# An attention-plus-MLP kernel: the states' readings gathered into two runs, their first layer on 512 columns, and identity transposes that nothing reads

## The chip, the cores and the metric

The kernel runs on one core of one Trainium2 chip. The metric is the device time of one execution in microseconds. The core's engines are TensorE (PE, matmuls; the profile lists its weight loads apart as PEld), VectorE (DVE), ScalarE (ACT), GpSimd (POOL, which here only builds the identity matrix) and SyncE (SP, which issues all transfers). Each works through its own queue in order and waits for the others by semaphores.

## What is computed

Eight batches of eight heads hold 512 tokens of width 64 (`x`) and 32 states of width 64 (`state`). Tokens attend to the states and states attend to the tokens; the results, 544 rows a batch of 512 columns, go through a gated MLP without a nonlinearity, (x w_a) * (x w_b) w_out, with an inner width of 1536.

```python
def _attn_ref(x, state):
    scores = scale * np.matmul(x, state.transpose(0, 1, 3, 2))
    a = softmax(scores)                      # max, exp, sum + 1e-9
    xread = np.matmul(a, state)
    scores2 = scale * np.matmul(state, x.transpose(0, 1, 3, 2))
    a2 = softmax(scores2)
    sread = np.matmul(a2, x)
    return np.concatenate([xread, sread], axis=2)

def _moe_ref(x, w_a, w_b, w_out):
    return ((x @ w_a) * (x @ w_b)) @ w_out
```

(`softmax` stands for the four lines of the original.) Everything is float32.

## The kernel before

**Precision.** Large products are made from pairs. An operand is split into a high part rounded to float32r and a low rest, and three matmuls, high by high, high by low and low by high, are added up. The weights come as 64-bit words and are put together by ACT (`pre`), DVE (`join`) and both (`run`) in `Conv`.

**The MLP of the tokens.** A batch's first layer needs no separate reading of the states: the normalised attention of the tokens (`at_h`, `at_l`) multiplies the states already projected through w_a and w_b (`p_h`, `p_l`). `VISITS` (line 32) lists which batch meets which of the six chunks of two feature tiles in which order; `SU` stands for the unit of all states, visited three times near the end. `layer1` (line 842) fills two `ab` tiles in PSUM, one for each half of the gate; ACT copies the first, DVE multiplies the second with it, and the product is split into `g_h` and `g_l`. `layer2` (line 863) follows two feature tiles later (`LAG`) and adds into `acc` tiles; the last feature tile of a visit is closed into `stg` and stored.

**The states' side.** `soft` and `moved` exponentiate a batch's scores and store them to a scratch in DRAM (`e_dram`). `reading` (line 530) fetches them in another layout (four transfers of 64 KB for each of two groups, `a2`) with the tokens (`xn`), multiplies both in 32 small float32 matmuls of 64 columns, `scaled` divides by the sums, two transposes (`turned`) turn the result and `keep` puts it into `xst`. Batch by batch, `attend` (line 916) lets a reading follow one batch behind the attention. A small float32 matmul has two records in the profile, so a reading has 64.

**The states' MLP.** `States.tokens` splits `xst` into two tiles. In `layer1` each feature tile has, for each gate half, 4 parts of depth by 3 products, 24 matmuls of 256 columns.

**The opening.** For batch 0 the scores of group 0 come from `x_raw` (PE into `ms`), those of group 1 from `stg` (PE into `ab`). ACT copies each, four identity transposes turn them, DVE and ACT make the softmax, and `at_h` and `at_l` follow. Only then can the stream of wide matmuls begin.

**The order of the work.** All calls are recorded as units and then issued in the order that the table `ORDER` (line 138) lists by number, for all engines at once:

```python
    with tc.manual_schedule():
        for i in arranged(rec.units):
            for obj, method, args, kw in rec.units[i].calls:
                getattr(obj, method)(*map(real, args), **{k: real(x) for k, x in kw.items()})
```

So each instruction has line 1078 in the profile, and groups are told apart by tiles. Tiles take their buffers from pools in that order; `ps_ab` and `ps_ms` have two banks each, `ps_acc` four.

Of the kernel before, what the change touches and what calls it, by code (L numbers as in the profile page):

```python
# [9 lines left out]
F32 = mybir.dt.float32  # L10
# [9 lines left out]
P = 128  # L20
TOK = S + NS
NG = 2
# [23 lines left out]
LATER, TWICE = 2, (3, 4)  # L46

BEHIND = 1
# [90 lines left out]
0 5 1 6 10-11 19 23 121-122 34 137 2 35 138 36 3-4 8 520-521 7 9 37 62 38 48 68 20-21 39 22 12 49 40 296 24-25 50 13  # L139
26 16 522 51 27 41 52 14 123 28 106 42 53 43 204 31 1060 17 44 63 54-56 45 57 15 46 64 58 47 70 32 65 74 59 75 525 76  # L140
66 29 77 60 523 69 107 61 67 524 18 526 71 80 108 78 206 79 124 530 109 33 125 86 110 81 30 82 205 126 83-84 1061 85
111 576 90-91 127 208 869 92-93 112 212 94 87 95 216 128 139 113 295 72 220 129 88 96 114 97 140 130 115 98 131 99 116
142 100 160 527 141 163 166 161 143 169 102 117 132 164 118 542 170 167 89 101 133 587 103 119 134 168 165 207 104 144
518 162 73 171 120 1063 135 150 528 136 200 188 145 209 590 210 529 146-147 214 1066 151 226 211 192-193 148 105 152
213 153 218 154 149 189 215 362 156 196 190 598 535 217 155 201 191 197 157 366 202 198 579 219 194 199 172 540 173
222 178 158 1062 179-180 221 232 195 370 870 223 581 174 233 175 253 235 176 582 234 177 256 184 259 159 260 181 203
236 182-183 224 237 536 257 185 227 238-239 531 240 228 532 261 241 229 254 262 225 243 230 242 255 363-364 297 231
249 378 186 368 374 244 533 258 245-246 537 534 247-248 599 263 284 250 287 264 365 288 251 265-266 836 267 367 837
187 268-269 298 271 369 384 272 300 270 578 299 281 371 290 541 291 301 285 277 286 282 372 292 588 327 373 1070
273-274 577 376 289 375 302 583 380 303 519 275 377 324 584 325 276 379 328 1079 283 390 381 278 382 304 386 391  # L150
305-306 252 393 307-308 392 309 314 318 310 279 394 311-312 385 538 313 330-331 387 332 543 315 1071 280 333 585 334
383 335 580 319 546 342 321 539 322-323 1064 544 336 395 326 591 562 329 316 354 547 388 320 346-347 358 548 348 355
349-350 563 351-352 545 560 356 337 357 338 564 339 411 552 359 340 353 341 396 549 397 343 360 412 839 398 561 344
389 399-400 568 401 317 586 345 569 402 592 414 550 361 403-404 407 1072 405 551 417 589 1073 413 789 439 406 1081 593
1080 423 408 424 565 425 594 426 596-597 427 1082 420 1068 421 418 553 415-416 595 442 409 1074 429-432 443 1083 428
1075 554 858 1084-1085 555 422 556 433 435 434 440-441 1086 436 448 419 410 449 1087 450 481 570 1065 451 557 445 452
444 475 454 476 453 446 558 472 456 455 477 437 457 1069 458-459 462-463 460-461 571 861 504 559 468 1110 572 464 1111
465-466 566 505 484-485 840 438 567 467 486 1088 600 469 293 1076 294 487 791 601 506 490 1097 603 491 602 492 825 447
830 493 604 488 478 831 479 489 482 496 473 494-495 470 474 483 497 480 828 605 471 500 498 501 606-607 502 667 790
573 507 574 611-612 668 832 575 499 613 512-513 503 608-609 826 859 610 669 614 617 621 1067 622 508 1077 827 615 1112  # L160
833 514 1090 1113 624 616 509 1078 510 618 625-626 670 633 639 619 1106 671 1089 634 511 640 635 1107 636 1091 637-638
641 620 645 642-644 1098 728 646 515 729 731 730 627 732 1099 653 672 678 673 679-680 674-676 623 1100 792 649 829 681
793 682 834 654 630 794-795 517 798 655 677 1154 628 811 629 684 657-658 809 1108 796 650 1109 651 631 683 652 647 659
632 700 685 701-702 797 703 661 688 799 706-708 704 648 800 705 662-663 810 656 814 709 664 710-712 835 660 713 1092
691 812 841 856 692 686 733 1160 1101 734 838 735 1122 736 801 737 694 842 697 847 738 845 844 698 846 843 852 699 802
725 855 739-740 803 1123 687 871 849 862 745 741 516 872 742 695 874 693 873 689 726 1125 714 743 875 744 853 696 804
722 746 761 723 854 938 813 1124 805 817 848 762 806 1093 763-764 719 1094 1155 767-769 807 1156 690 770 716 1102-1103
717 1157 765 771 766 808 939 772 718 749 941 815 724 755 1095 756 940 816 757 720 1096 851 818 750-751 850 727 1104
942 758 1227 759 1116 1162 1105 715 721 752 747 753 783 1161 748 1114 777 819 1115 778 820 784 821 779 1117 1126 892
754 773 822 1127 780-781 760 774 786 823 785 1120 824 876 1118 1163 877 1119 878 882-883 1121 1128 884 879 775 1129  # L170
857 1228 1236 1164 1130 860 863 885 1131 880-881 864 787 2160 1132 866 865 776 1146 788 1133 901 868 902 867 2171 886
888 1165 1147 887 893 1245 1134 889 2165 782 1135-1136 665 904 1148 1137 905 910 1166 906 890 907 666 999 891 1254
1149 911 1158 912-914 1159 1229-1230 915 908-909 894 916 895-897 1000 920-921 1002 1231 922 917 943 1232 898 944 1001
945 1237 903 1233 932-933 923 946 1238 899 1234 900 1239 1140 1235 947 1003 949-950 1246 1311 1247 948 951 1240 955
924 952-953 918 954 959 1241 1138 956 928 1248 1139 971 977-978 1141 1242 925 929 1151 930 1249 1243 979 1256 1150 926
934 2126 927 1142 1144 936 1143 1735 960 1255 972 2168 931 962 980-981 1257 961 935 987 973 1258 974 1250 937 919 982
975-976 1145 965 963 983 1153 968-969 1312 984 1152 970 1265 1167 1251 1004 966 1244 967 1313 1010 1263 1252 1314 1253
1315 1317 996 1005 988 1006 1264 964 1007-1008 957 1279 993-994 1266 958 995 1011-1012 1280 1013-1014 1384 1259-1260
1015 1271 1009 1272-1273 990 1261 1283 1026-1028 1016 1267 1274 989 1017 1020 985 997 1319 991 1268 1032-1034 1318
1038 1035 1169 1269 1320 1393 998 1168 1270 1287 1039 1170 1262 1282 1040 992 1281 986 1029 1288-1289 1316 1030 1290  # L180
1036 1275 1386 1321 1021-1022 1385 1031 1057 1276-1277 1387 1018 1041 1285 1037 1388 1293 1278 1048 1389-1390 1286
1049 1042 1019 1284 1043-1044 1050 1303 1187 1394 1188 1045 1304 1023 1291 1391 1322 1171 1024 1392 1172 1395
1173-1174 1396 1292 1402 1025 1175 1294 1177 1397 1178 1323 1179 1398-1399 1180 1058-1059 1400 1176 1051-1052 1401
1181-1182 1053 1183 1411 1196 1295 1305 1299 1306 1296 1197 2162 1198 1300 1054-1055 1046 1309 1056 1297 1047 1199
1298 1301 1184 1224 1403 1193 1404 1190 1302 1405 1185 1200 1310 1413 1201 1324 1202 1420 1203 1191 1326 1325 1192
1194 1421-1422 1406 1195 1436 1423 1204-1205 1424 1437 1206 2167 1307 1425-1426 1308 1207 1211 1221 1438 1222 1412
1208 2166 1209 1328 1407-1408 1414 1329-1330 1327 1409 1331 1210 1218 1212 1415 1410 1219 1186 1189 1225 1427 1468
1226 1353-1354 1416 1439 1332 1417 1430 1334 1418 1335-1336 1428 1419 1220 1347 1429 1333 1223 1431 1350-1351 1213
1441 1432 1440 1434 1433 1348-1349 1435 1442 1375 1215 1443-1444 1541 1474 1216 1445 1337 1734 1338-1340 1217 1355
1341 1381 1352 1450 2172 1214 1342 1356-1357 1469-1470 1448 1343 1480 1358 1449 1344 2163 1362 1376 1451 1543 1359  # L190
1452 1360 2373 1361 1382 1460 1368 1383 1510 1446 1378 1447 1363-1365 1453 1461 1366 1454 1463 1379 1464 1455 1380
1507 1462 1508 1481 1377 1465 1504 1483 1505 1367 1544 1345-1346 1369 1546 1458 1476 1456 1482 1372 1511 1484-1486
1491 1471 1487 1612 1488-1489 1545 1475 1490 1492-1493 1497 2382 1494-1495 1370 1542 1496 1373 1457 1374 1498 1513
1459 1501 1466 1371 1512 1499 1519 2124 1467 1506 1547 1472 1532 2125 1533 1520 1477 1673 1538-1539 1500 1509 1478
1534 1514 1473 2374 1515-1516 1535 2375 1536 1517 2376 1518 1521 1525 1522 2377 1523 1537 1613 1524 1570 1548 1526
# [144 lines left out]
def attn_moe(ctx, tc, xt, xn, sd, wl, w_out, out):  # L340
# [13 lines left out]
    proj = pool("proj", 2)  # L354
    att = pool("att", 2)
    mlp = pool("mlp", 2)
    tail = pool("tail", 8)
# [763 lines left out]
```

## Time and profile before

| | us |
|---|---|
| median of 3 runs | 669.06 |
| lowest and highest | 668.98, 669.69 |
| the profiled execution | 669.0 |
| its span, first to last instruction | 667.2 |
| PE busy | 655.5 (98%), 3760 matmul records |
| DVE busy | 425.9 (64%), 811 instructions |
| ACT busy | 377.4 (57%), 699 instructions |
| transfers | 122.71 MB in the main queue, 55.3% of 16 DMA engines' span |

Times in the profile count from the span's start. A matmul's recorded duration includes its way through the array, so neighbours overlap; what one costs in a stream is the distance of the starts. "Idle before" is the time an engine stood still ahead of an instruction, and the name behind it is what ended that.

### The profile page before, as it was taken

To read this page: it belongs to the slowest core of one execution; us is meant where nothing else is said; L and a number is where in the kernel's file an instruction comes from. 1 tells how busy PE (TensorE), PEld (TensorE's weight loads), DVE (VectorE), ACT (ScalarE), POOL (GpSimd) and SP (SyncE) were. 2 spreads that over 40 slices of the span, in tenths; PEclk is the share of its full clock that TensorE was granted. 3 is DMA by queue.
4 is the path that set the end of the run, shared out by engine and by line. 5 is a ranking of instruction groups with operands and counts; after the bars stand their busy time and mean duration, and the time that the engine had idled before them with its cause. 6 is when DMAs were issued, how large, how long until landed. Compare 5 with 4: busy or idle time off the path is not lost.

```text
span 667.2 us, 10159 instructions
## 1 busy us (share of the span) xinstructions
PE 655.5 (98%) x3760; PEld 524.8 (79%) x3760; DVE 425.9 (64%) x811; ACT 377.4 (57%) x699; POOL 0.7 (0%) x6
## 2 busy tenths in 40 slices
PE   5999999999999999999999999999999999999997
PEld 1677777778888887888787878888888888888886
DVE  5989978856743756787867876744455544564332
ACT  4886744669986777675565543533345344543321
POOL 0000000000000000000000000000000000000000
PEclk9999999999999999999999999999999999999999
DMA  9798164688789764969978733454034330341002
GB/s 314 255 303 279 61 210 142 233 261 293 263 286 335 273 189 146 305 199 294 314 260 271 241 129 128 143 190 151 7 115 155 110 111 1 120 163 49 0 1 94
DMA packets 59632, 123.34 MB, mean 185 GB/s; under 512 B 9920, under 2 KB 18112, under 8 KB 59584
## 3 DMA queue, kind: packets, MB, share of 16 engines
q1 hardware_dynamic: 59584, 122.71, 55.3%
q8 instruction: 29, 0.48, 0.3%
q14 instruction: 19, 0.16, 0.1%
HBM read 85.46 MB, written 37.22 MB: 184 GB/s over the span
## 4 chain that ended last, share of the span: by engine, by line
PE 98%; DMA 1%; SPq 0%; DVE 0%; ACT 0%; issue 0%
PE ab L1078 45%; PE acc L1078 42%; PE ms L1078 10%; DMA stg<-xt 1%; SPq L1078 0%; DVE stg L1078 0%; ACT at_h L1078 0%
## 5 line engine op out<-in xcount | busy, mean ns | idle before, releaser
L1078 PE MATMUL acc<-wo,g_h 128*128 128x512 f32 x816 | 265.1, 391 | 0.0
L1078 PEld LDWEIGHTS acc<-wo,g_h 128*128 128x128 f32 x816 | 152.1, 188 | 33.5 <-issue 2.5
L1078 PE MATMUL acc<-wo,g_l 128*128 128x512 f32 x408 | 152.4, 391 | 0.0
L1078 DVE TENSOR_TENSOR a_sb<-ab,a_sb 128x512 f32<-128x512 f32 (+1 forms) x108 | 71.0, 657 | 125.4 <-PE ab L1078 83.2
L1078 PE MATMUL ab<-at_l,p_h 128*128 128x512 f32 x384 | 148.7, 392 | 0.0
L1078 PE MATMUL ab<-at_h,p_h 128*128 128x512 f32 x384 | 147.2, 392 | 0.0
L1078 PE MATMUL ab<-at_h,p_l 128*128 128x512 f32 x384 | 147.0, 391 | 0.0
L1078 ACT COPY a_sb<-ab 128x512 f32<-128x512 f32 (+1 forms) x108 | 60.9, 564 | 113.5 <-PE ab L1078 97.9
L1078 ACT CAST g_h<-a_sb 128x512 fp32r<-128x512 f32 (+1 forms) x108 | 64.7, 599 | 64.6 <-PE acc L1078 32.6
L1078 DVE TENSOR_TENSOR g_l<-a_sb,g_h 128x512 fp32r<-128x512 f32 (+1 forms) x108 | 70.4, 654 | 37.1 <-ACT g_h L1078 25.2
L1078 PEld LDWEIGHTS acc<-wo,g_l 128*128 128x128 f32 x408 | 76.4, 188 | 15.3
L1078 PEld LDWEIGHTS ab<-at_h,p_h 128*128 128x128 f32 x384 | 72.1, 188 | 19.4 <-issue 2.1
L1078 PEld LDWEIGHTS ab<-at_h,p_l 128*128 128x128 f32 x384 | 72.1, 188 | 18.4 <-issue 3.8
L1078 PEld LDWEIGHTS ab<-at_l,p_h 128*128 128x128 f32 x384 | 72.1, 188 | 17.3 <-issue 2.5
L1078 DVE TENSOR_TENSOR p_l<-p_raw,p_h 128x512 fp32r<-128x512 f32 x72 | 47.9, 682 | 20.5 <-ACT p_h L1078 20.5
L1078 DVE SCALAR_TENSOR_TENSOR t<-t,t 128x512 int32<-128x512 int32 x60 | 41.4, 689 | 21.1 <-ACT t L1078 19.9
L1078 ACT CAST p_h<-p_raw 128x512 fp32r<-128x512 f32 x72 | 43.3, 620 | 8.3 <-PE ab L1078 4.9
L1078 ACT ACTIVATE t<-raw 128x512 f32<-128x512 f32 x42 | 28.2, 671 | 10.7 <-DMA raw<-wl 5.1
L1078 ACT COPY sw_st<-ms 128x512 f32<-128x512 f32 x40 | 22.9, 587 | 10.4 <-PE ms L1078 10.1
L1078 PE MATMUL ms<-wq,sd_h 128*128 128x512 f32 x72 | 28.1, 391 | 0.0
L1078 PE MATMUL ms<-wq,sd_l 128*128 128x512 f32 x72 | 28.0, 389 | 0.0
L1078 ACT COPY stg<-acc 128x512 f32<-128x512 f32 x34 | 19.7, 589 | 12.5 <-PE acc L1078 12.4
(121 smaller groups left out, 628.3 us busy)
## 6 DMA issues: line engine op xcount, KB each, us to landing
p_raw<-scr SPq DMA_DIRECT2D x36, 512.0 KB, 5.0
raw<-wl SPq DMA_DIRECT2D x34, 512.0 KB, 5.3
scr<-sw_st SPq DMA_DIRECT2D x40, 256.0 KB, 5.1
out<-stg SPq DMA_DIRECT2D x34, 256.0 KB, 4.8
scr<-wo SPq DMA_DIRECT2D x32, 256.0 KB, 4.4
wo<-wl SPq DMA_DIRECT2D x10, 512.0 KB, 5.9
x_raw<-xt SPq DMA_DIRECT2D x8, 576.0 KB, 5.6
raw<-w_out SPq DMA_DIRECT2D x8, 512.0 KB, 5.4
```

What stands on the lines that cost most here:

```text
L1078: getattr(obj, method)(*map(real, args), **{k: real(x) for k, x in kw.items()})
```

## The change

Four things change in the program, and the table `ORDER` is written anew for all of it.

1. `reading` takes four batches. After visit 9 (`READ`) it reads batches 0 to 3, ahead of the states' unit batches 4 to 7; the readings in `attend` go. The fetched tiles take buffers named `raw`, `sw_st`, `sd_h`, `sd_l` and `wq`. The 256 small matmul records of four batches are one unit; two batches share one bank, and their transposes come in groups of four.
2. `tokens` puts high and low part side by side, and `States.layer1` multiplies the high weights by both in one matmul of 512 columns, the low weights by the high part in one of 256. The right half of the bank holds the second product and is added to the left by an ACT copy and a DVE addition.
3. `unread` puts 13, 4, 8 and 4 transposes of the identity ahead of batch 0's two score groups and their transposes, into the bank that is overwritten next.
4. In the last visit of the states, the second row block is computed in two column halves with an `acc` tile each, closed and stored apart.

```diff
-LATER, TWICE = 2, (3, 4)
-BEHIND = 1
+LATER = 2
+UNREAD = {(0, 0): (13, 4), (0, 1): (8, 4)}
+READ = {9: (0, 1, 2, 3)}
...
 ORDER = """
-0 5 1 6 10-11 19 23 121-122 34 137 2 35 138 36 3-4 8 520-521 7 9 37 62 38 48 68 20-21 39 22 12 49 40 296 24-25 50 13
...
-    def reading(b):
-        gs = [atts[b, g] for g in range(NG)]
-        for a, name in zip(gs, ("x_raw", "x_nat")):
-            a.fetch(name)
-        ps = ps_ms.tile([P, 512], F32, name="ms")
+    def reading(batches):
+        gs = [(i, atts[b, g]) for i, b in enumerate(batches) for g in range(NG)]
+        for i in range(4):
+            name, bufs = ("raw", 2) if i < 2 else ("sw_st", 2)
+            t = proj.tile([P, NG, 4, 4, 32], F32, name=name, bufs=bufs)
+            for _, a in gs[2 * i:2 * i + 2]:
+                name, bufs = (f"sd_{'hl'[a.g]}{i}", 1) if i < 2 else ("wq", 4)
+                a.fetch(t[:, a.g], proj.tile([P, 4, 256], F32, name=name, bufs=bufs))
+        ps = [ps_ms.tile([P, 512], F32, name="ms") for _ in range(2)]
         with rec.together():
-            for a in gs:
+            for i, a in gs:
+                a.s, x = ps[i // 2], (2 * (i % 2) + a.g) * D
                 for sb in range(4):
...
-        for a in gs:
-            a.s = ps
-            a.scaled(a.g * D)
...
+        for half in (gs[:4], gs[4:]):
+            for i, a in half:
+                a.scaled((2 * (i % 2) + a.g) * D)
+            with rec.together():
+                for i, a in half:
+                    a.turned((2 * (i % 2) + a.g) * P)
...
+        def unread(self, k, ps):
+            for _ in range(UNREAD.get((self.b, self.g), (0, 0))[k]):
+                nc.tensor.transpose(ps[:, :P], ident, ident)
...
+        def layer1(self, ft):
+            both = []
+            for ab in range(2):
+                ps = ps_ab.tile([P, 512], F32, name="ab")
+                for k in range(4):
+                    x = self.rhs(k)
+                    wh, wlo = self.lhs(ft, k, ab)
+                    nc.tensor.matmul(ps, lhsT=wh, rhs=x.rearrange("p a n -> p (a n)"), start=(k == 0), stop=(k == 3),
+                                     skip_group_check=True)
+                    nc.tensor.matmul(ps[:, :self.n], lhsT=wlo, rhs=x[:, 0], start=False, stop=(k == 3), skip_group_check=True)
+                both.append(ps)
+            n = self.n
+            g, t = [mlp.tile([P, 512], F32, name="a_sb") for _ in range(2)]
+            nc.scalar.copy(out=g, in_=both[0])
+            nc.scalar.copy(out=t[:, n:], in_=both[1][:, n:])
+            nc.vector.tensor_tensor(out=g[:, :n], in0=g[:, :n], in1=g[:, n:], op=ALU.add)
+            nc.vector.tensor_tensor(out=t[:, :n], in0=both[1][:, :n], in1=t[:, n:], op=ALU.add)
+            return g[:, :n], t[:, :n]
...
-            for k, (l, r) in enumerate(((gh, 0), (gh, 1), (gl, 0))):
-                nc.tensor.matmul(u.acc[i], lhsT=l[:, ts], rhs=wo[ft][:, r],
-                                 start=(first and k == 0), stop=(last and k == 2))
-            if last:
-                u.close(i, u.acc[i], final)
+            halves = final and u is units[SU] and i == nt - 1
+            for h in range(2 if halves else 1):
+                cols, ps = (slice(256 * h, 256 * h + 256), u.acc[i + h][:, :256]) if halves else (slice(0, DM), u.acc[i])
+                for k, (l, r) in enumerate(((gh, 0), (gh, 1), (gl, 0))):
+                    nc.tensor.matmul(ps, lhsT=l[:, ts], rhs=wo[ft][:, r, cols],
+                                     start=(first and k == 0), stop=(last and k == 2))
+                if last:
+                    u.close(i, ps, final, cols)
...
-            while pending:
-                reading(pending.pop(0))
+            reading((4, 5, 6, 7))
             unit.tokens()
...
+        if v in READ:
+            reading(READ[v])
```

How the rewritten table moves instructions is seen on PE at three places. The first is the start of PE's queue, the opening (`wo` holds batch 0's copied scores, `p_raw` converted weights, `p_h` products). Before:

```order
L1078 MATMUL ms<-x_raw 32x512 x4
L1078 MATMUL ms<-ident,wo_123 128x128 x4
L1078 MATMUL ab<-stg 32x512 x4
L1078 MATMUL acc<-p_raw,x_raw 32x256 x4
L1078 MATMUL acc<-p_raw,stg 32x256 x4
L1078 MATMUL ab<-ident,wo_123 128x128 x4
L1078 MATMUL acc<-p_raw,x_raw 32x256 x4
L1078 MATMUL acc<-p_raw,stg 32x256 x4
L1078 MATMUL acc<-p_h,wo_94 128x256
```

and now:

```order
L1109 MATMUL ms<-ident 128x128 x13
L1109 MATMUL ms<-x_raw 32x512 x4
L1109 MATMUL ms<-ident 128x128 x4
L1109 MATMUL ms<-ident,wo_128 128x128 x4
L1109 MATMUL ab<-ident 128x128 x8
L1109 MATMUL ab<-stg 32x512 x4
L1109 MATMUL acc<-p_raw,x_raw 32x256 x4
L1109 MATMUL acc<-p_raw,stg 32x256 x4
L1109 MATMUL ab<-ident 128x128 x4
L1109 MATMUL ab<-ident,wo_128 128x128 x4
L1109 MATMUL acc<-p_h,wo_132 128x256
```

The unread transposes stand ahead of each score group and of each group's four transposes, and the first product's rest (`acc<-p_h`) comes ahead of the second products.

The second place is a reading: before, one of eight, between wide matmuls of a batch (`x_raw` and `x_nat` hold the tokens, `a` the fetched exponentials):

```order
L1078 MATMUL ab<-at_l,p_h 128x512
L1078 MATMUL ab<-at_h,p_l 128x512
L1078 MATMUL ab<-at_h,p_h 128x512
L1078 MATMUL ms<-x_raw,a_321 32x64 x16
L1078 MATMUL ms<-x_nat,a_540 32x64 x16
L1078 MATMUL ab<-at_l,p_h 128x512
L1078 MATMUL acc<-wo_568,g_h 128x512
```

and now the first of the two runs:

```order
L1109 MATMUL ab<-at_h,p_l 128x512 x2
L1109 MATMUL acc<-wo_1577,g_h 128x512
L1109 MATMUL ms<-sd_h_3186,raw 32x64 x16
L1109 MATMUL ms<-sd_l_3153,raw 32x64 x16
L1109 MATMUL ms<-sd_h_3511,raw 32x64 x16
L1109 MATMUL ms<-sd_l_3559,raw 32x64 x16
L1109 MATMUL ms<-wq,sw_st 32x64 x64
L1109 MATMUL acc<-wo_1614,g_l 128x512
L1109 MATMUL ab<-at_h,p_h 128x512
```

128 small matmuls stand in a row where 32 stood, with the tokens in `sd_h`, `sd_l` and `wq`, the exponentials in `raw` and `sw_st`.

The third place is in the second visit of the states, with buffer numbers and the semaphores waited for (`x_nat` and `x_raw` are the states' tokens, `ab_5890` is the second gate half of a feature tile, `ab_5915` belongs to the next):

```order
L1109 MATMUL acc_5407<-wo11_2367,g_h_5779 128x512
L1109 MATMUL acc_5884<-wo4_793,g_l_5822 128x512
L1109 MATMUL ab_5890<-x_nat_5053,wq_5726 128x256
L1109 MATMUL ab_5890<-x_raw_4976,wq_5574 128x512
L1109 MATMUL ab_5890<-x_raw_4976,wq_5726 128x256
L1109 MATMUL ab_5890<-x_raw_4976,wq_5574 128x512
L1109 MATMUL ab_5915<-x_nat_5053,wq_5843 128x512 [waits PE_49,Activation_49]
L1109 MATMUL ab_5890<-x_raw_4976,wq_5726 128x256 [waits Activation_49]
L1109 MATMUL acc_5407<-wo11_2367,g_l_5785 128x512
L1109 MATMUL acc_5923<-wo4_793,g_h_5818 128x512
```

The last 256-column matmul into `ab_5890` waits for ACT, which copies the right half of that bank; one other matmul stands between it and the last of 512 columns.

## Rows read from the trace of the kernel before

**Rows 1.** The page, part 4: the chain that ended last, by engine.

```profile
PE 98%; DMA 1%; SPq 0%; DVE 0%; ACT 0%; issue 0%
```

**Rows 2.** Stretches: us, each engine's busy us, PEclk, DMA share, GB/s.

```profile
4.34:10.09 5.75, 3.02 (x13) 0.94 (x13) 2.70 (x6) 1.81 (x3) 0.00 (x0) 1.00 0.97 343
10.09:14.00 3.91, 3.91 (x28) 1.14 (x28) 3.67 (x8) 2.73 (x7) 0.00 (x0) 1.00 1.07 385
14.00:18.00 4.00, 3.41 (x31) 1.26 (x30) 3.86 (x10) 3.09 (x9) 0.00 (x0) 1.00 1.03 363
30.00:667.00 637.00, 633.36 (x3604) 513.20 (x3602) 403.63 (x765) 357.05 (x658) 0.00 (x0) 1.00 0.54 180
```

**Rows 3.** PE's waits, first and last of four: total us, times, longest.

```profile
PE ms L1078 <- DMA x_raw<-xt: 4.3, 1, 4.3
...
PE ms L1078 <- ACT at_h L1078: 0.7, 1, 0.7
```

**Rows 4.** Timeline of PE around a reading: start us, us, operation, count.

```profile
69.52 0.39 PE L1078 MATMUL ab<-at_h,p_h 128*128 128x512 f32 x1
69.83 0.65 PE L1078 MATMUL ms<-x_raw,a 128*32 128x64 f32 x32
70.31 0.63 PE L1078 MATMUL ms<-x_nat,a 128*32 128x64 f32 x32
70.86 0.50 PE L1078 MATMUL ab<-at_l,p_h 128*128 128x512 f32 x1
71.20 0.40 PE L1078 MATMUL acc<-wo,g_h 128*128 128x512 f32 x1
```

**Rows 5.** Timeline of PE around a pair of result transposes.

```profile
383.86 0.38 PE L1078 MATMUL ms<-ident,a 128*128 128x128 f32 x2
...
384.54 0.40 PE L1078 MATMUL acc<-wo,g_l 128*128 128x512 f32 x1
```

**Rows 6.** Pieces of the chain in order of time: start us, us, what.

```profile
430.76 4.99 PE acc L1078 x22
...
482.88 0.24 PE acc L1078
...
484.52 2.98 PE ab L1078 x25
```

**Rows 7.** Groups by shape on ACT: count, busy us, mean ns, idle before.

```profile
L1078 ACT COPY a_sb<-ab 128x512 f32<-128x512 f32 x96 | 56.4, 587 | 96.2 <-PE ab L1078 80.6 <-DVE g_l L1078 10.4 <-DVE m L1078 3.0
...
L1078 ACT COPY a_sb<-ab 128x256 f32<-128x256 f32 x12 | 4.5, 373 | 17.3 <-PE ab L1078 17.3
```

**Rows 8.** Timeline of the opening: start us, us, what, idle before, releaser.

```profile
1.01 0.29 POOL masks.py:199 TENSOR_SCALAR_AFFINE_SELECT ident<-ident 128x128 f32<-128x128 f32 x1
...
4.35 1.93 PE L1078 MATMUL ms<-x_raw 128*32 128x512 f32 x8 [4.35 <-DMA x_raw<-xt]
...
6.82 0.43 DVE L1078 TENSOR_SCALAR t<-raw 128x512 int32<-128x512 uint32 x1 [6.82 <-DMA raw<-wl]
...
8.10 1.08 PE L1078 MATMUL ms<-ident,wo 128*128 128x128 f32 x4 [1.82 <-ACT wo L1078]
...
10.09 1.94 PE L1078 MATMUL ab<-stg 128*32 128x512 f32 x8 [0.90 <-DMA stg<-xt]
...
13.01 1.10 PE L1078 MATMUL ab<-ident,wo 128*128 128x128 f32 x4
...
14.38 0.68 DVE L1078 TENSOR_REDUCE m<-ab 128x16 f32<-128x512 f32 x1
...
15.40 1.07 PE L1078 MATMUL ms<-stg 128*32 128x512 f32 x8
```

**Rows 9.** Groups by shape on PE: the transposes of the first scores.

```profile
L1078 PE MATMUL ms<-ident,wo 128*128 128x128 f32 x4 | 1.1, 424 | 1.8 <-ACT wo L1078 1.8
```

**Rows 10.** The tail's timeline, and GB/s in 40 slices of 655:668.

```profile
663.39 0.69 DVE L1078 TENSOR_TENSOR stg<-acc,stg 128x512 f32<-128x512 f32 x1 [1.12 <-PE acc L1078]
...
GB/s 271 0 0 0 0 0 0 0 0 0 0 0 315 410 82 0 0 0 120 403 403 410 277 0 0 365 403 38 0 0 139 403 265 0 0 0 0 0 0 0
```

More of the change, by code (lines that the diff above doesn't have):

```diff
@@ L144 @@
[L144 to L148, printed above, removed]
@@ L356, in attn_moe @@
     mlp = pool("mlp", 2)
-    tail = pool("tail", 8)
+    tail = pool("tail", 15)
     dram = pool("dram", 1, space=bass.MemoryType.DRAM)
@@ L539, in reading @@
                         n = at(a.g, hq)
-                        nc.tensor.matmul(ps[n * NS:(n + 1) * NS, a.g * D:(a.g + 1) * D], lhsT=a.a2[:, n, sb],
+                        nc.tensor.matmul(a.s[n * NS:(n + 1) * NS, x:x + D], lhsT=a.a2[:, n, sb],
                                          rhs=a.xn[:, sb, hq * D:(hq + 1) * D], start=(sb == 0), stop=(sb == 3))
-        for a in gs:
-            a.s = ps
-            a.scaled(a.g * D)
-        with rec.together():
-            for a in gs:
-                a.turned(2 * P + a.g * P)
-        for a in gs:
-            a.keep(2 * P + a.g * P)
+        for half in (gs[:4], gs[4:]):
[4 more added lines that the diff above has]
+                    a.turned((2 * (i % 2) + a.g) * P)
+            for i, a in half:
+                a.keep((2 * (i % 2) + a.g) * P)
     def new_a(b):
@@ L586, in scores @@
             with rec.together():
+                self.unread(0, self.s)
                 for hq in range(4):
@@ L599, in scores_t @@
             with rec.together():
+                self.unread(1, self.t)
                 for sb in range(4):
@@ L662, in moved, with fetch @@
                               in_=t.rearrange("p (q x) -> p q x", q=4))
-        def fetch(self, name):
-            self.a2 = att.tile([P, 4, 4, 32], F32, name="a2", bufs=2)
-            self.flat = self.a2.rearrange("p a b c -> p (a b c)")
+        def fetch(self, a2, room):
+            self.a2, self.xn = a2, room
+            self.flat = a2.rearrange("p a b c -> p (a b c)")
             for q in range(4):
-                nc.sync.dma_start(out=self.a2[q * 32:(q + 1) * 32].rearrange("t h k n -> t h (k n)"),
+                nc.sync.dma_start(out=a2[q * 32:(q + 1) * 32].rearrange("t h k n -> t h (k n)"),
                                   in_=e_dram[self.b, self.g][:, :, q].rearrange("h t x -> t h x"))
-            self.xn = att.tile([P, 4, 256], F32, name=name, bufs=1)
-            nc.sync.dma_start(out=self.xn, in_=xn[self.b, self.g])
+            nc.sync.dma_start(out=room, in_=xn[self.b, self.g])
         def scaled(self, x):
@@ L814, in tokens @@
             xs = xst.rearrange("p h b n -> p h (b n)")
-            self.x = [att.tile([P, 4, B * NS], F32R, name=n, bufs=1) for n in ("x_nat", "x_raw")]
-            nc.scalar.copy(out=self.x[0], in_=xs)
-            minus(nc.vector, self.x[1], xs, f32(self.x[0]))
+            self.x = [att.tile([P, 2, 2, B * NS], F32R, name=n, bufs=1) for n in ("x_nat", "x_raw")]
+            for j, x in enumerate(self.x):
+                r = xs[:, 2 * j:2 * j + 2]
+                nc.scalar.copy(out=x[:, :, 0], in_=r)
+                minus(nc.vector, x[:, :, 1], r, f32(x[:, :, 0]))
         def lhs(self, ft, k, ab):
@@ L822, in rhs, with close @@
         def rhs(self, k):
-            return [t[:, k, :] for t in self.x]
-        def close(self, i, acc, final):
+            return self.x[k // 2][:, k % 2]
+        def layer1(self, ft):
[16 more added lines that the diff above has]
+            return g[:, :n], t[:, :n]
+        def close(self, i, acc, final, cols):
             if not self.begun:
@@ L830, in close @@
             else:
[L831 removed]
+                nc.vector.tensor_tensor(out=self.sums[:, i, cols], in0=acc, in1=self.sums[:, i, cols], op=ALU.add)
             if final:
                 r = B * S + i * P
[L834 to L835 removed]
+                o = self.sums[:, i, cols]
+                nxt.append(lambda: nc.sync.dma_start(out=out[r:r + P, cols], in_=o))
             if i == 1:
@@ L842, in layer1 @@
     def layer1(u, ft):
-        res = []
-        for ab in range(2):
-            ps = ps_ab.tile([P, 512], F32, name="ab")
-            m = 0
-            for k in range(u.nk):
-                xh, xl = u.rhs(k)
-                wh, wlo = u.lhs(ft, k, ab)
-                for a, b in ((wh, xh), (wh, xl), (wlo, xh)):
-                    nc.tensor.matmul(ps[:, :u.n], lhsT=a, rhs=b, start=(m == 0), stop=(m == 3 * u.nk - 1))
-                    m += 1
-            res.append(ps)
-        g = mlp.tile([P, 512], F32, name="a_sb")[:, :u.n]
-        nc.scalar.copy(out=g, in_=res[0][:, :u.n])
-        nc.vector.tensor_tensor(out=g, in0=res[1][:, :u.n], in1=g, op=ALU.mult)
+        if u is units[SU]:
+            g, t = u.layer1(ft)
+        else:
+            res = []
+            for ab in range(2):
+                ps = ps_ab.tile([P, 512], F32, name="ab")
+                m = 0
+                for k in range(NG):
+                    xh, xl = u.rhs(k)
+                    wh, wlo = u.lhs(ft, k, ab)
+                    for a, b in ((wh, xh), (wh, xl), (wlo, xh)):
+                        nc.tensor.matmul(ps, lhsT=a, rhs=b, start=(m == 0), stop=(m == 3 * NG - 1))
+                        m += 1
+                res.append(ps)
+            g, t = mlp.tile([P, 512], F32, name="a_sb"), res[1]
+            nc.scalar.copy(out=g, in_=res[0])
+        nc.vector.tensor_tensor(out=g, in0=t, in1=g, op=ALU.mult)
         gh = mlp.tile([P, 512], F32R, name="g_h", bufs=LAG + 1)[:, :u.n]
@@ L866, in layer2 @@
         if first:
-            u.acc = [ps_acc.tile([P, 512], F32, name="acc") for _ in range(nt)]
+            u.acc = [ps_acc.tile([P, 512], F32, name="acc") for _ in range(nt + bool(final and u is units[SU]))]
         fill = list(fill)
@@ L938, in attend @@
                 a.back()
-        if b not in WIDE:
-            pending.append(b)
-            for _ in range(2 if b in TWICE else 1):
-                if len(pending) > BEHIND:
-                    reading(pending.pop(0))
     def afterwards(b):
@@ L1043, in attn_moe @@
                     ready.add(b)
-            while pending:
-                reading(pending.pop(0))
+            reading((4, 5, 6, 7))
             unit.tokens()
```

370 lines of the change are left out of this document (186 added, 184 removed).

## The prediction

> **What bounds the kernel now.** First I read the chain that ended last: 98% of the span is TensorE (PE), whichever tile it works for [rows 1]. Then the stretches: from 30 us to the end PE is busy 633.36 of 637.00 us and the other 3.6 are the tail, whose last addition starts at 663.39 [rows 10], while DVE and ACT are free for a third of that time and more [rows 2]. The list of PE's waits has four entries, the largest 4.3 us for the first input, another for ACT's `at_h` [rows 3], none after the opening. So the span is three pieces: an opening of some 20 us in which PE waits for the first inputs and for DVE's and ACT's softmax work, a gapless stream of matmuls, and a tail. In the stream every step that PE saves is saved from the end, and work moved along the stream is worth what its shape costs there, no more.
>
> The sum is made against the profiled execution, 669.0 us (span 667.2 and 1.8 around it); the median of the runs is 669.06. What a measurement can tell from no change is 0.2%, 1.3 us.
>
> **Readings in two runs.** One batch's reading is 64 recorded small matmuls. In the rows the wide matmul before starts at 69.52, the first small one at 69.83, the second half at 70.31, the next wide ones at 70.86 and 71.20 [rows 4]. So 69.52 to 71.20 holds one reading and two wide steps of 0.23 [rows 6], and the reading costs 1.68 - 0.46 = 1.22 us. Of that, 0.48 passes from the first small one to the 33rd, at most 0.96 for 64; the other 0.26 at least is paid for switching: 0.08 extra on the way in (0.31 for 0.23), the rest on the way out and on the wide matmul behind. The first half holds one slow first round of its own, so I put the 64 at 0.91 and the switching at 0.31. The second half shows no extra gap at its start, though it reads other tiles. Eight readings pay the switching eight times; two runs of four pay it twice: 6 x 0.31 = **-1.86 us** (bounds 6 x 0.26 = -1.6 and, if a half is 0.45, 6 x 0.32 = -1.9). The loads and stores behind them keep their number: 64 small fetches and 16 of `xn`, now issued in two clusters. The pairs of result transposes become groups of four: a pair and two wide steps take 383.86 to 384.54 [rows 5], so a pair costs 0.68 - 0.46 = 0.22, about 0.11 each, and joining pairs gives nothing I can see. I cost it at 0.
>
> **States' first layer.** Per feature tile 24 matmuls of 256 columns become 8 of 512 and 8 of 256. A run of 25 at 256 took 2.98, 0.119 each; a run of 22 at 512 took 4.99, 0.227 each; a 512 that stands between 256s took 0.24 [rows 6]. Twenty-four at 0.119 are 2.86. With 0.227 the new mix is 1.82 + 0.95 = 2.77, 0.09 less; with 0.24 it is 2.87, 0.01 more. The new order has wide and narrow mixed, but in one bank and with layer 2's wide ones around, so I take 0.23: 2.79, 0.07 less, twelve times: **-0.8 us** (bounds -1.1 and +0.1). For this ACT and DVE get an additional copy and two additions per feature tile. They have room on average, so I price them only where PE waits for them.
>
> **A new wait.** In four of the 24 state tiles the built order puts ACT's copy of the right half ahead of the tile's last 256-column matmul, which then waits for ACT. Between the 512 that completes the right half and that matmul stand 3, 6, 1 and 12 others. With one between (the place shown for `ab_5890`), the 512 needs 0.39 from start to end as a wide one does [rows 4], the copy 0.373 [rows 7], and PE has 2 x 0.23 to do meanwhile: 0.39 + 0.37 - 0.46 = **+0.3 us**. With three between nothing is left. Bounds: 0, and 4 x 0.3 = 1.2 if ACT comes to all four late. Behind that matmul stand layer 2's wide ones, so the delay goes to the end whole.
>
> **Halves in the last states visit.** In four feature tiles, three 512s become six 256s: 6 x 0.119 - 3 x 0.227 = 0.03 each [rows 6], **+0.14 us**. At the very end the left half is complete 8 x 0.119 = 0.95 us before PE ends, so its addition and its store are out of the way. The last addition has half the columns. The whole one takes 0.69 [rows 10], a 256-column DVE addition is not among the rows; ACT's copies go from 0.587 to 0.373 [rows 7], so I take 0.2 to 0.3 less. The last store is 128 KB for 256; at the peak of 410 GB/s [rows 10] that is up to 0.3 less, and at least 0 if its fixed part rules. Together **-0.45 us** (bounds -0.2 and -0.6).
>
> **The unread transposes.** The opening's first eight scores took 1.93, the second eight 1.94, and the same shape at 15.40 took 1.07 [rows 8]: early PE runs at the lower of its two levels (1.2 for 2.4 GHz), though the granted clock in the stretches reads 1.00 from 4.34 on [rows 2]. Ahead of the change to the full rate PE was busy 3.91 of 3.91 us; before that, 3.02 of 5.75 without a change. The 29 transposes fill PE's idle time. If that brings the full rate some 5 us earlier, the second scores and the four transposes behind them shrink by 1.94 - 1.07 = 0.87 and by some 0.4 us. But this is not the end of a chain: DVE begins at 6.82, when the first weights land [rows 8], and from there to 18.00 it is busy 2.70 + 3.67 + 3.86 = 10.23 of 11.18 us. PE's stream starts when DVE has normalised and ACT has split the first attention. The number of DVE steps ahead of that is the same. So the gain is at most DVE's 0.95 idle us, and the likeliest is **0**: what PE finishes earlier waits for DVE, which is late next. On the other side, the transposes stand in PE's queue. At the lower rate one takes (1.08 - 0.42) / 3 = 0.22 us [rows 8, 9]. Thirteen from the end of `ident` (1.30) on last until 4.2, ahead of the first input; four and four, then eight, end near 9.9, ahead of 10.09. Only the last four, behind the products, would stand in the way at that rate: 0.9 us, of which 0.3 is slack before DVE's reduction at 14.38. Bounds: -0.95 and +0.6.
>
> Sum: -1.86 + 0 - 0.8 + 0.3 + 0.14 - 0.45 + 0 = -2.67, so **666.3 us**.
>
> **Rivals.** (a) The opening gives all of DVE's idle time as well: 666.3 - 0.95 = 665.4. For it: some of those gaps end on PE's or ACT's work. Against: 0.57 of it (3.27 less 2.70) falls before 10.09, while the weights arrive and ahead of the second scores. (b) Unread transposes do not raise PE's rate: +0.6, 666.9. Rows can't exclude it: the busy stretch that ended in the full rate held four transposes at 13.01 but also 24 score and product records [rows 2, 8]. The Trainium skill ("TensorE: Matmul & The Clock Gate", Part 4 on the PE-mode transpose) says that transposes do not count as a busy PE for the clock. By that rule (b) is what happens; no row here has a stretch of transposes alone, so no run yet shows it. (c) The slower side: the states' visits become bound by ACT's copies. A state tile is now free only after a 512-column copy, or a half copy and an addition, with two banks to alternate. If each of 24 tiles held PE 0.3 us as the one above, that is 7.2 - 0.3 more: 673.2. It decides from 14 tiles on (14 x 0.3 = 4.2, against the 2.7 gained and 1.3 for a visible loss). Against it: ACT is free 44% of the stream [rows 2], and layer 2 stands between most tiles. (d) The change does not do what it says: the runs' 40 fetches each come late and PE waits, or the switching is paid at every batch inside the run. Either takes back up to 1.86: 668.2. Against: no matmul of the stream waited for a transfer [rows 3], and rows 4 show a change of tiles without a gap.
>
> **Numbers.** The forecast case 0.55, (a) 0.14, (b) 0.2, (c) 0.04, (d) 0.07. The range reaches from the better bounds of readings and first layer together with part of (a), 665.0, to (b) with a larger wait, 667.9; the ends beyond, 664.5 and (c) and most of (d), are left out with 2 in 10. Faster by over 0.2% means under 667.7: the forecast case but for its worst bounds, (a), and most of (b), 0.81. Within 0.2%: the rest of (b), (d) and part of the bounds, 0.15. Slower: (c), 0.04.
>
> **What would show it.** Right: two stretches of 256 small records of some 3.6 us, each with one slow step in and out; 0.09 us or less gained per states' feature tile; one PE wait for ACT of about 0.3 us near the states' second visit and none else in the stream; last addition some 0.2 to 0.3 shorter; the stream of wide matmuls beginning as before within 0.5 us. Wrong: PE waits for a transfer in front of a run, state tiles waiting one after the other, an opening that moves by over 1 us, or a stream step that is no longer 0.227.

## The result and the profile after

The changed kernel takes 673.45 us (median of 6, 671.85 to 673.88) against 669.10 for the one before, a ratio of 1.0058 [1.0045, 1.0071]: slower by 0.58%, where 666.3 and a gain were forecast. Its profiled execution took 673.52 us, span 671.7 (before: 667.2). Of the 11 executions of the kernel without unread transposes, below, one took 1129.84 us at a mean granted clock of 0.627; it is left out of that kernel's ratio, and without it the median would be 669.94.

The first view, the list of PE's waits, which answers to [rows 3] (us in total, times, longest), has a new first line:

```profile
PE ms L1109 <- issue: 4.3, 2, 2.3
PE ab L1109 <- DMA stg<-xt: 1.6, 1, 1.6
PE ms L1109 <- POOL ident masks.py:199: 1.4, 1, 1.4
PE ms L1109 <- PE acc L1109: 0.9, 1, 0.9
PE ab L1109 <- ACT wo L1109: 0.7, 1, 0.7
PE ms L1109 <- ACT at_h L1109: 0.6, 1, 0.6
PE ab L1109 <- ACT a_sb L1109: 0.2, 1, 0.2
PE acc L1109 <- ACT p_h L1109: 0.2, 1, 0.2
```

"Issue" is time in which PE waits for nothing that the profile shows. Both times stand inside the two runs. PE's timeline through the first run, against [rows 4], and the end of the second:

```profile
348.30 0.39 PE L1109 MATMUL acc<-wo,g_h 128*128 128x512 f32 x1
348.62 0.65 PE L1109 MATMUL ms<-sd_h,raw 128*32 128x64 f32 x32
...
350.43 1.73 PE L1109 MATMUL ms<-wq,sw_st 128*32 128x64 f32 x106
354.49 0.54 PE L1109 MATMUL ms<-wq,sw_st 128*32 128x64 f32 x22 [2.33 <-issue]
354.95 0.50 PE L1109 MATMUL acc<-wo,g_l 128*128 128x512 f32 x1
355.29 0.39 PE L1109 MATMUL ab<-at_h,p_h 128*128 128x512 f32 x1
...
441.16 1.31 PE L1109 MATMUL ms<-wq,sw_st 128*32 128x64 f32 x78
444.44 0.97 PE L1109 MATMUL ms<-wq,sw_st 128*32 128x64 f32 x50 [1.97 <-issue]
...
447.07 0.63 PE L1109 MATMUL acc<-wo,g_l 128*128 128x512 f32 x1
447.50 0.63 PE L1109 MATMUL acc<-wo,g_h 128*128 128x512 f32 x1
```

The first run stops after 128 + 106 = 234 of its 256 matmuls, the second after 206, in the middle of a batch. From start to start the two holes are 2.55 and 2.19 us. Behind the second, wide matmuls follow each other at 0.43 instead of 0.227; the stretch (columns as in [rows 2]) has half the granted clock, 1.2 GHz:

```profile
446.03:449.44 3.41, 3.41 (x10) 2.63 (x9) 1.91 (x5) 1.72 (x7) 0.00 (x0) 0.50 0.09 34
```

That costs another 1.5 us, and not always: four executions of six have a mean granted clock of 0.995 to 0.997 and take 673.39 to 673.88, the two at 1.000 take 671.85 and 672.09. Only for the profiled one of the four does a trace show where the stretch lies.

Where the time went, from three points of both traces: PE's stream of wide matmuls begins at 19.01 (before 19.23), its last matmul starts at 668.26 (662.97), the span ends at 671.74 (667.21). So the opening gives 0.22, the tail 0.76, and the stream takes 649.25 instead of 643.74, 5.51 more. Of these 2.55 + 2.19 are the holes and 1.5 the half clock; without them the stream is some 0.7 shorter than before.

What PE waits for in the holes no wait names, but the page's list of DMA queues points at it. One queue carries instructions in 29 transfers (packets, MB, share):

```profile
q8 instruction: 29, 0.48, 0.3%
```

They are of 16384 bytes each. PE's own instructions are 3,705 matmuls, as many weight loads and 68 for semaphores and drains, 7,478 recorded, and 29 x 256 = 7,424. Kernels of the experiments that give PE 256 and 512 instructions more than the kernel before (which has 29 too) have 30 and 31 such transfers. So the queue is PE's, and a transfer is a block of 256 instructions. In the stream 256 instructions are 128 wide matmuls, 29 us; in a run they are 128 small ones at 0.0141, 1.8 us. In the first hole, 352.2 to 354.49, the same list has one block:

```profile
q8 instruction: 1, 0.02, 2.5%
```

It is transferred from 352.24 to 353.17, begun when PE had already stopped, and PE goes on at 354.49. At the second hole a block is transferred from 441.55 to 443.01; PE's last matmul ahead of the hole starts at 442.25, the next at 444.44. Counted along PE's recorded instructions, the holes stand behind number 4,033 and number 5,313, which are 1,280, or five blocks, apart.

### The profile page after: what moved, and what is told of

Same layout as the page of the kernel before. It is cut to its first block, busy times and chain, and to the rows that moved or that the text cites. A ratio compares the mean times of both kernels' runs of the same rounds, so it can differ in the third digit from the quotient of the medians.

```text
span 671.7 us, 10081 instructions
## 1 busy us (share of the span) xinstructions
PE 658.6 (98%) x3705; PEld 525.9 (78%) x3705; DVE 438.4 (65%) x837; ACT 383.5 (57%) x712; POOL 0.7 (0%) x6
## 4 chain that ended last, share of the span: by engine, by line
PE 97%; DMA 1%; issue 1%; ACT 0%; SPq 0%; DVE 0%; ACTq 0%
PE ab L1109 45%; PE acc L1109 42%; PE ms L1109 10%; DMA wo<-wl 1%; SPq L1109 0%; ACT t L1109 0%; ACT at_h L1109 0%; ACT s_p L1109 0%; DVE stg L1109 0%; ACT a_sb L1109 0%; ACT p_h L1109 0%; ACT wo L1109 0%; ACTq L1109 0%
## 5 line engine op out<-in xcount | busy, mean ns | idle before, releaser
L1109 PE MATMUL acc<-wo,g_h 128*128 128x512 f32 (+1 forms) x824 | 268.7, 389 | 0.0
L1109 PEld LDWEIGHTS acc<-wo,g_h 128*128 128x128 f32 x824 | 153.9, 188 | 34.9 <-issue 2.9
L1109 PE MATMUL acc<-wo,g_l 128*128 128x512 f32 x412 | 154.9, 391 | 0.0
L1109 ACT COPY a_sb<-ab 128x512 f32<-128x512 f32 x120 | 67.9, 567 | 106.0 <-PE ab L1109 91.5
L1109 ACT CAST wq<-raw 64x512 fp32r<-64x512 f32 x40 | 24.7, 618 | 5.7 <-DVE raw L1109 3.0
```

## The experiments

My theory: PE's instruction supply. A run is 512 short instructions in a row, used up faster than a block arrives. Rivals: the runs' 40 transfers (the prediction's (d)), and the other parts of the change.

| kernel | median us | ratio to before [95%] |
|---|---|---|
| runs in 4 pieces | 670.23 | 1.0017 [1.0008, 1.0026] |
| runs in 2 pieces | 668.46 | 0.9994 [0.9985, 1.0003] |
| no unread transposes | 670.08 | 1.0015 [1.0006, 1.0024] |
| 2 pieces, none unread | 668.29 | 0.9988 [0.9979, 0.9997] |
| states' 512 split | 674.27 | 1.0070 [1.0057, 1.0083] |
| before + 128, one strip | 683.69 | 1.0219 [1.0203, 1.0234] |
| before + 64, one strip | 676.63 | 1.0112 [1.0098, 1.0126] |
| before + 128, batch 4 | 674.47 | 1.0081 [1.0065, 1.0096] |
| before + 64, batch 4 | 670.91 | 1.0028 [1.0018, 1.0039] |
| before + 64, batch 5 | 671.85 | 1.0040 [1.0026, 1.0054] |
| 2 pieces, orders mended | 667.92 | 0.9985 [0.9976, 0.9993] |
| the same, none unread | 667.68 | 0.9983 [0.9974, 0.9992] |

**Runs in pieces.** The issuing loop cuts a run and sets its earlier pieces `k` PE units ahead of the next:

```diff
+def spread(plan, pieces, k):
+    out = list(plan)
+    for u in [u for u in plan if len(u.calls) == 128]:
+        n, size = out.index(u), 128 // pieces
+        out.pop(n)
+        for j in reversed(range(pieces)):
+            p = Unit("PE")
+            p.calls = u.calls[j * size:(j + 1) * size]
+            out.insert(n, p)
+            seen = 0
+            while j and seen < k:
+                n -= 1
+                seen += out[n].eng == "PE"
+    return out
...
-        for i in arranged(rec.units):
+        for u in spread([rec.units[i] for i in arranged(rec.units)], 4, 8):
```

> The changed kernel, but each run of four batches is issued in four pieces of one batch (64 recorded matmuls), eight matmul instructions of the stream between one piece and the next, so the first piece stands about 5 us earlier. Theory (instruction supply): in the changed kernel TensorE stops inside each run for 2.3 and 2.0 us because its instructions come from memory in blocks of 16 KB, 256 instructions of 64 bytes, and 512 short ones in a row are used up faster than a block arrives. In pieces no stop is left and no stretch at half clock follows; six more switches at 0.24 us each come back. 673.45 - 4.3 to 4.8 - 1.0 to 1.7 + 1.4 gives 668 to 670. Rival A (the runs' 40 small transfers come late, or disturb): pieces that start earlier wait for their tiles, TensorE waits for DMA, 673 or more. Rival B (the loss lies in the states' first layer, in the halves or in the opening): the time stays within 1 us of 673.45 less what the half clock cost.

With `2, 12` in place of `4, 8`:

> The changed kernel, each run in two pieces of two batches (128 recorded matmuls, 256 instructions with their weight loads), twelve matmul instructions (2.7 us) between. Theory (instruction supply): a block lasts 1.8 us in a piece and the next one needs some 4 us from being called for to being used, so the wide ones between and around have to cover about 2 us: mostly they do. Stops of 0 to 1 us in all, two more switches (0.5 us): 667.5 to 669.5, at or below the four pieces. Rival A (late transfers): as late as in the changed kernel or later, 672 or more. Rival B (other parts): 671 to 673.

Neither shows a wait for issue. In two pieces (PE's timeline) all 128 of each go through:

```profile
347.77 0.63 PE L1125 MATMUL ms<-sd_l,raw 128*32 128x64 f32 x32
...
351.28 1.99 PE L1125 MATMUL ms<-wq,sw_st 128*32 128x64 f32 x128
353.21 0.50 PE L1125 MATMUL acc<-wo,g_l 128*128 128x512 f32 x1
```

Four pieces began too early for their data (timeline of that kernel), so rival A is real there, at 0.6 us, but only there:

```profile
345.99 0.65 PE L1125 MATMUL ms<-sd_l,raw 128*32 128x64 f32 x32 [0.60 <-DMA raw<-e_dram]
```

With this wait in it, the kernel with four pieces lies 0.2 above the range expected of it.

Cutting a run once gives 5.0 us back with every other part of the change in place: rival B, as the cause of the loss, falls.

**Moving the holes.** `UNREAD = {}` takes 58 instructions away ahead of everything.

> The changed kernel without the 29 unread transposes (29 matmul and 29 load instructions fewer ahead of everything). Theory (instruction supply): blocks are cut by instruction count, so each call for a block comes 58 instructions later in the run. The first stop, after 468 of 512 instructions in the changed kernel, then falls at 526, seven wide matmuls behind the run's end, and shrinks from 2.3 to about 0.7 us; the second moves from 412 to 470 instructions (235 matmuls) into its run and keeps its 2 us. The opening at the lower clock costs 0 to 0.6. Together 672 to 673.2. Rival A (late transfers): both stops stay at the same matmul of the run, 673.5 to 674. Rival C (the opening's clock matters): the stream starts later by up to 0.9 us and nothing else moves, 674.

PE's timeline, behind the first run and in the second:

```profile
353.75 0.39 PE L1109 MATMUL ab<-at_h,p_h 128*128 128x512 f32 x1
354.92 0.40 PE L1109 MATMUL ab<-at_l,p_h 128*128 128x512 f32 x1 [0.78 <-issue]
...
439.62 1.73 PE L1109 MATMUL ms<-wq,sw_st 128*32 128x64 f32 x105
443.00 0.54 PE L1109 MATMUL ms<-wq,sw_st 128*32 128x64 f32 x23 [1.64 <-issue]
```

The first hole now stands behind the run, ahead of a wide matmul for which the profile shows no wait on a tile: six wide ones run between the run's last and the hole, where seven were expected. The second stands after 128 + 105 = 233 matmuls instead of 206 (235 expected). Both moved by the instructions removed: along PE's instructions they stand behind number 4,032 and number 5,312, to within one where they stood in the changed kernel, with other work there. So block borders set the place, not tiles or the runs' transfers. The time, 670.08, is 2 us below what I expected: from start to start the holes shrank to 1.17 and 1.86, and the ten executions counted have a mean clock of 0.999 or 1.000, none with the half clock's 0.997 or less.

Both edits together:

> Two pieces of 128 to a run, and the unread transposes left out. The 58 instructions fewer ahead move the call for a block from 212 instructions into the first run to 270, that is 14 into its second piece; by theory (instruction supply) 242 short ones and seven wide matmuls then have to last the 4.1 us that a block needs, they last 3.3, and a stop of about 0.8 us comes back some seven wide matmuls behind the first run's second piece, none in the second run. The opening begins the stream up to 0.3 us earlier. 668.5 to 669.2. Rival (stops depend on the row's length alone): no stop, 668.0 to 668.4.

The expected hole did not come: the next block's transfer began at 352.42, with the second piece rather than after it. How long a block needs from being called for is not in the trace, and my 4.1 us was too long here. The time is the one that the rival gives, so this run does not tell the theory from a stop that goes by the row's length; the rows below do. The 0.17 us to the kernel with two pieces lies within the scatter.

**Rows without transfers.** Kernel before, with unread matmuls of the constant identity ahead of one batch's scores:

```diff
         with rec.together():
+            for k in range(128 if b == 5 else 0):
+                nc.tensor.matmul(gs[0].s[:32, :64], lhsT=ident[:, :32], rhs=ident[:, :64], start=True, stop=True)
             for hp in range(2):
```

> The kernel before, with 128 unread fp32 matmuls (64 columns, 32 columns of weights, both from the identity; 256 recorded ones, 512 instructions with their loads, as in a run of the change) put ahead of the scores of batch 5. They read a constant tile, so no transfer and no other engine can hold them. Theory (instruction supply): 256 x 0.0141 = 3.6 us of work, some 0.2 for the switch, and one stop of 1.6 to 2.6 us wherever the block border falls, marked as waiting for issue: 674.5 to 675.5. Rival A (the stops belong to the transfers or tiles of the readings): no stop, 3.8 us more, 672.9.

> As the kernel with 128 unread matmuls, but 64 of them (128 recorded, 256 instructions: one block). Theory (instruction supply): 1.8 us of work and 0.2 for the switch, and no stop unless the block border falls within the first 20 or so instructions of the row: 671.0. Rival A' (a stop that grows with the length of the row): half of what 128 of them cost, 672.1.

Both theories failed in the price: all write one strip of 32 partitions, and so take 0.0555 each (256 in 14.2 us), not 0.0141; 128 of them cost 14.5 and 64 half, 7.4. As a control it still serves: 512 instructions at a quarter of the pace show no wait for issue, so neither the number nor the form of the instructions stops PE, the pace must come in. Going round four strips (`n = k % 4 * 32`, output `gs[0].s[n:n + 32, :64]`) they run at the readings' pace:

> The kernel before with 128 unread fp32 matmuls ahead of the scores of batch 4, again from the identity alone, but going round the four strips of 32 output partitions as the readings do, so that they run at the readings' pace. Theory (instruction supply): 256 recorded at 0.0141 = 3.6 us, 0.2 for the switch, and a stop marked as issue. By the blocks' transfers in the trace of before (one at 252.6 us; in the changed kernel TensorE ran dry 499 instructions behind the start of the last one) it comes some 420 of 512 instructions into the row, after about 210 matmuls, and lasts 1.6 to 2.5 us: 674.6 to 675.5. Rival A (the readings' transfers): no stop, 673.0.

> As with 128 ahead of batch 4, but 64 of them: 256 instructions, over 160 short of where TensorE would run dry. Theory (instruction supply): no stop, 1.8 + 0.2: 671.1. Rival A' (a stop with every row of this length, in proportion): half of what 128 cost.

> The same 64 matmuls ahead of the scores of batch 5, the same work at another place. There the last transfer of a block ahead of it (293.2 us) puts the point of running dry some 240 of 256 instructions into the row or just behind it. Theory (instruction supply): a stop of 1.5 to 2.3 us, at about 120 matmuls or within a few wide ones behind the row: 672.5 to 673.4, 1.5 to 2.3 more than the same row ahead of batch 4. Rival (a stop depends on how long the row is): the same time as at batch 4.

PE's timelines: 128 ahead of batch 4, then 64 there, then 64 ahead of batch 5.

```profile
260.23 3.43 PE L1081 MATMUL ms<-ident 128*32 128x64 f32 x229
265.13 0.64 PE L1081 MATMUL ms<-ident 128*32 128x64 f32 x27 [1.47 <-issue]
```

```profile
260.38 1.99 PE L1081 MATMUL ms<-ident 128*32 128x64 f32 x128
262.30 0.62 PE L1081 MATMUL ms<-x_raw 64*32 64x512 f32 x2
```

```profile
321.40 1.99 PE L1081 MATMUL ms<-ident 128*32 128x64 f32 x128
...
325.10 0.50 PE L1081 MATMUL acc<-wo,g_h 128*128 128x512 f32 x1 [0.69 <-issue]
```

No transfer and no other engine is in these rows, yet 128 stop PE for 1.7 us after 229 (210 expected). 64 do not ahead of batch 4 and do ahead of batch 5, 0.94 us dearer in the median for the same work. There the hole stood 16 score matmuls behind the row and was 0.7 us, smaller and later than expected. Along PE's instructions these two holes stand behind number 3,521 and number 4,033: two blocks apart, and the second at the very number of the changed kernel's first hole, though other instructions stand there. Rival A falls, and so does a stop that goes by length alone.

**The first layer.** Each 512-column matmul as two of 256:

```diff
-                    nc.tensor.matmul(ps, lhsT=wh, rhs=x.rearrange("p a n -> p (a n)"), start=(k == 0), stop=(k == 3),
-                                     skip_group_check=True)
+                    with rec.together():
+                        for i in range(2):
+                            nc.tensor.matmul(ps[:, i * self.n:(i + 1) * self.n], lhsT=wh, rhs=x[:, i],
+                                             start=(k == 0), stop=(k == 3), skip_group_check=True)
```

> The changed kernel with each 512-column matmul of the states' first layer issued as two of 256 columns in a row, copies and additions as in the change. It prices the term of the first layer alone: 96 times (2 x 0.119 - 0.227) = +1.0 us by the prediction's prices, 674.5, both stops unmoved since these visits lie behind both runs. If the first layer saved nothing: 673.4. Rival B (the loss lies in these visits, state tiles waiting for copies): smaller pieces change the waits by more than 1.5 us either way.

0.8 more in the median, though the two intervals overlap. Its stream without the holes (2.59 and 1.64) is 643.8 against 643.0 for the changed kernel without holes and half clock: 0.8 again.

**A better version.** Two pieces, and the two orders that made PE wait:

> Two pieces of 128 to a run with the unread transposes in place, and two orders mended: ACT's copy of the right half comes behind the last 256-column matmul of its state tile wherever it stood ahead of it, and one DVE subtraction that stood ahead of the last four copies out of the first run's second bank comes behind them. By the changed kernel's trace the first wait is 0.39 us, the second (the scores behind the run, which need that bank) 0.58. 668.46 - 1.0 gives 667.5; if the copies are late anyway or another wait takes their place, 668.0 to 668.5.

> Two pieces to a run, both orders mended, and no unread transposes. Between the kernels with two pieces their removal gave 0.17 us; here the same: 667.6 to 667.9, with fewer runs that show a stretch at half clock in the opening. If the unread transposes help where nothing else waits: 668.2 or more.

667.92 and 667.68. In the first the wait for `a_sb` is gone from the list, and the scores behind the run take the 1.02 that they take elsewhere; its stream is 642.81 against 643.74 for pieces alone, 0.93 of the 0.97 that the two waits were worth. I expected 667.5 of it, and 667.6 to 667.9 of the second. Both are faster than the change, and than the kernel before by 0.15 and 0.17%; between the two the difference is within the scatter.

## Why the prediction was wrong, point by point

- **Readings in two runs, -1.86: the step that failed.** It took the pace of 64 matmuls and the lack of a gap at the 33rd [rows 4] for 256 in a row, and so put the supply of PE's instructions at nothing. Rival (d) asked only whether the fetched data would be late or the switching come more often. The page's instruction queue was not read, so no bound for 512 instructions in 3.6 us was set. The saving itself is there: from 348.30 to 355.29 less the hole and two wide steps are 3.98 us, 0.9 less than four readings of 1.22; twice, 1.8. The holes cost 4.7, more than twice what the runs save.
- **States' first layer, -0.8:** right; splitting it back costs 0.8.
- **The new wait, +0.3:** right; one of the four tiles, a step of 0.62 instead of 0.23, so 0.39. PE held by ACT's copy of the right half, in the timeline:

```profile
577.39 0.40 PE L1109 MATMUL ab<-x_nat,wq 128*128 128x512 f32 x1
577.59 0.37 ACT L1109 COPY a_sb<-ab 128x256 f32<-128x256 f32 x1 [1.58 <-PE ab L1109]
...
578.02 0.39 PE L1109 MATMUL ab<-x_raw,wq 128*128 128x256 f32 x1 [0.23 <-ACT a_sb L1109]
```

- **A wait that no term had: +0.6.** A run holds both `ms` banks until DVE has copied its results out. The scores behind the first run find the second bank in use (DVE's last four copies and the scores in the timeline): 16 of them take 1.60 where they otherwise take 1.02. With two pieces alone they still take 1.60; with one DVE subtraction moved behind the copies as well this wait is gone.

```profile
364.29 0.69 DVE L1109 TENSOR_TENSOR g_l<-a_sb,g_h 128x512 fp32r<-128x512 f32 x1
...
365.01 0.83 DVE L1109 COPY xst<-ms 64x64 f32<-64x64 f32 x4
...
365.40 1.05 PE L1109 MATMUL ms<-x_raw 64*32 64x512 f32 x4
365.98 0.62 PE L1109 MATMUL ms<-x_nat,s_p 64*32 64x512 f32 x2
```

- **Halves and tail, +0.14 - 0.45:** right in sign, too small in size. The last addition takes 0.42 instead of 0.69 as priced, against [rows 10]:

```profile
668.57 0.42 DVE L1109 TENSOR_TENSOR stg<-acc,stg 128x256 f32<-128x256 f32 x1 [0.53 <-PE acc L1109]
```

From the last matmul's start to the end 4.24 became 3.48: 0.76 less, where 0.6 was the better bound. Not priced: the copy and additions of the last feature tile come late to their own layer 2, some 0.2 us of PE's time ahead of the end:

```profile
665.89 0.30 PEld L1109 LDWEIGHTS acc<-wo,g_h 128*128 128x128 f32 x2 [0.33 <-ACT g_h L1109]
```

- **Unread transposes, 0:** right for the opening as far as the traces tell. The stream began at 19.01, in four other traces with unread transposes at 19.15 to 20.52, in the kernel before and the rows added to it at 18.91 to 19.44. Two things that they did besides were not thought of. They moved every block border by 58 instructions. And the half clock goes with them: the mean clock is 0.997 or less in 20 of 44 executions of the five kernels that have them, with holes or without, and in none of the 32 counted of the three kernels with the change's readings that lack them. In the changed kernel it cost 1.5. In two pieces the trace has it in the opening, and there executions with it (668.04 to 669.47) are not dearer than those without (667.96 to 669.80).

Without holes and half clock the span would be 671.7 - 4.7 - 1.5 = 665.5, the time 667.3: inside the range, 1.0 above the forecast, and the two waits without a term, 0.6 and 0.2, are most of that 1.0; the rest lies in steps too small to name. Slower came by a mechanism that no rival named; (c), given 0.04, had the sign but neither place nor price.

## What to carry to other kernels

Before putting short matmuls into one row, count instructions, weight loads included, against the instruction queue's blocks: here 256 to a block, and a row of 512 at 7 ns each ran dry within it or just behind it at every place tried, one of 256 at one place only, and cutting a row of 512 once with twelve wide matmuls between left no hole. "Issue" inside a row without dependences is the line to look for, and any edit that changes the number of instructions ahead moves it. A joined step also holds its buffers longer: ask who needs the next one.

## What had not been expected of the hardware

- **Instruction blocks.** The Trainium skill ("Runtime: NRT & Kernel Launch", Instruction fetch mechanics) says that the sequencer fetches instructions in blocks of 16 KiB, 256 of them, on its own queue; the trace agrees (29 transfers of 16384 bytes, and eight holes in five kernels at places 512, 1,280 or 1,792 instructions apart, to within one, which are multiples of 256). It also says that crossing a block is mostly hidden: for wide matmuls it is, for rows at 7 ns an instruction it cost up to 2.6 us here, and nothing at some borders.
- **Transposes and the clock.** With two pieces, 13 unread transposes are all that PE did before the first scores, and those eight take 1.10 us; without unread transposes they take 1.94 (PE's timelines of the two openings):

```profile
1.36 3.03 PE L1125 MATMUL ms<-ident 128*128 128x128 f32 x13 [1.36 <-POOL ident masks.py:199]
4.36 1.10 PE L1125 MATMUL ms<-x_raw 128*32 128x512 f32 x8
```

```profile
4.30 1.94 PE L1109 MATMUL ms<-x_raw 128*32 128x512 f32 x8 [4.30 <-DMA x_raw<-xt]
```

The rule of the Trainium skill that the prediction weighed ("TensorE: Matmul & The Clock Gate", Part 4), that transposes do not count as a busy PE for the clock, does not hold in this execution. In the other four traces with unread transposes the eight scores take 1.45, 1.61, 1.73 and 1.94. The trace's first record of the full clock comes at 4.49 to 7.01 us in these five, at 12.22 to 19.21 in the nine traces without. But the early full rate need not last: in the opening with two pieces the granted clock reads 0.50 (1.2 GHz) again for 3.4 us, and the stream started at 19.47.

```profile
11.32:14.73 3.41, 3.41 (x37) 2.08 (x41) 3.00 (x8) 2.52 (x6) 0.00 (x0) 0.50 1.07 394
```

- **One strip or four.** The same small matmul takes 0.0555 us when all write one strip of 32 output partitions and 0.0141 when they go round four.
- **Open:** why the half clock comes with the unread transposes, in some executions only and at different places (11.32, 15.71 and 446.03 us in three traces), and how long before its transfer a block is called for. Neither was tried.
